# Early tile loads for the last gradient stage, one eviction moved from VectorE to ScalarE, and two stores freed of their order, in a gated linear-attention training kernel

## The chip, the cores and the metric

The kernel runs on one core of one Trainium2 chip. The metric is the device time of the execution in microseconds (us). The granted clock is the share of TensorE's full clock that the chip allows it, as the profile records it.

## The reference, cut to what matters

The reference is a forward pass and all its gradients. A gate `g` mixes two branches over `x` of 2048 rows and 640 columns: linear attention with 32 heads of 20, and a two-layer network with 1728 hidden columns.

```python
g = sigmoid((x * gate_w).sum(-1, keepdims=True))
a = linear_attention(x, wqkv) @ wo        # pq, pk = phi(q), phi(k); kv = pk^T v; z = sum pk
b = relu(x @ w1) @ w2                     # o = (pq kv) / (pq z + 1e-6)
out = g * a + (1 - g) * b
out, vjp = jax.vjp(f, x, wqkv, wo, w1, w2, gate_w)
return (out, *vjp(grad_out))              # d x, d wqkv, d wo, d w1, d w2, d gate_w
```

## The kernel before

The program is a sequence of phases over 16 tiles of 128 rows: 1 (k, v and the attention state), 2 (q, both branches, the output `po`), 3 and 4 (gradients of `w2` and `wo`, mixed with the attention gradient), 5 (hidden gradient), 6 (gradient of `w1`), 7 (gradients of q, k, v and of `x`), 8 (gradients of `wqkv` and of the gate). A scheduler orders the instructions of each engine, and buffers come from pools. An eviction (`evac`) copies a result that TensorE left in a PSUM buffer to an SBUF buffer, on ScalarE (`act`) or on VectorE (`dve`). A buffer of a released pool is used again by a later pool, and the later one then waits for the last use of the earlier one.

The end of a tile in phase 2. Three DMA transposes of the hidden tile and one of the attention tile leave as a burst, and the stores wait until the burst has landed:

```python
gT_ins = nc.sync.dma_start_transpose(goT[:], go_t[:])          # last of the four transposes
...
s1 = nc.gpsimd.dma_start(qkv_d[ts_, 0:D], pq_s[:])
tc.add_manual_dep(s1.ins, gT_ins.ins.name, sync_, reason="stores after the tile's transposing DMA burst")
s2 = nc.gpsimd.dma_start(go_d[ts_, :], go_t[:])
...
s3 = nc.gpsimd.dma_start(o_out[ts_, :], o_sb[:])
if t + 1 in lastT_p2:
    tc.add_manual_dep(s3.ins, lastT_p2[t + 1].ins.name, sync_, ...)
```

Phase 6, and the start of a tile in phase 7 (`p7_stage1`). Phase 7 has three stages, one tile apart each; stage 2 is the long one, with 30 matmuls into `pdx`:

```python
# phase 6, for each of five column blocks m
pw = ps4.tile([P, 2048], F32, tag="b4")
...                                                    # 64 matmuls
o_sb = w6p.tile([P, F], BF)
nc.scalar.copy(o_sb[:, 0:1024], pw[:, 0:1024])
nc.vector.tensor_copy(o_sb[:, 1024:F], pw[:, 1024:F])
nc.gpsimd.dma_start(out_4[m * P:(m + 1) * P, :], o_sb[:])
...
# phase 7
w7s = p7.enter_context(tc.tile_pool(name="w7s", bufs=2, side="right"))
w7p = p7.enter_context(tc.tile_pool(name="w7p", bufs=3, side="right"))
def p7_stage1(t):
    qkv_t = w7p.tile(...); nc.sync.dma_start(qkv_t[:], qkv_d[ts_, :])
    dndT_t = w7p.tile(...); nc.sync.dma_start(dndT_t[:], dndT_d[t])
    ...                                                # 6 transposes of k into PSUM: ppk
    evac("act", pkT[:], ppk[:])
    ...                                                # 6 transposes of v into PSUM: pvt
    evac("dve", vT[:], pvt[:])
    nc.vector.tensor_scalar(ep[:], qkv_t[:, 0:2 * D], -EPS, 1.0, ALU.add, ALU.min)
    ...                                                # pdq = dndT KVZt, pdv = pkT dKVz, pdk = vT dKVzt
    nc.vector.tensor_tensor(dq_t[:, 0:D], pdq[:, 32:32 + D], ep[:, 0:D], ALU.mult)
    nc.scalar.copy(dq_t[:, 2 * D:3 * D], pdv[:, 32:32 + D])
    nc.vector.tensor_tensor(dq_t[:, D:2 * D], pdk[:, 32:32 + D], ep[:, D:2 * D], ALU.mult)
def p7_stage1b(t): ...                                 # 15 transposes of dq_t (pt_, pt), evicted to dqT
def p7_stage2(t): ...                                  # pdx: 30 matmuls, then dx_sb and its store
p7_stage1(0); p7_stage1(1); p7_stage1b(0)
for t in range(NT):
    if t + 2 < NT: p7_stage1(t + 2)
    if t + 1 < NT: p7_stage1b(t + 1)
    p7_stage2(t)
```

## Time and profile before

| | |
|---|---|
| time, 4 runs | 802.33 us median, 800.47 to 805.8 |
| profiled run | 800.47 us, of which 798.8 us from the first to the last instruction |
| TensorE busy | 724.2 us, 91% of the span |
| phase 7, tile after tile | 6.953 us each |
| from the last matmul to the end | 20.4 us |

In the lines of a profile PE is TensorE and PEld its weight loads, DVE is VectorE, ACT is ScalarE, POOL is GpSimd, SPq is the queue of transfers that SyncE issues, and L602 is line 602 of the kernel. The first parts of the profile's page show busy time, the busy tenths in 40 slices of the span, and the share of each engine in the chain of work that ended last.

```profile
PE 724.2 (91%) x5410; PEld 426.2 (53%) x5507; DVE 311.0 (39%) x603; ACT 181.9 (23%) x291; POOL 94.9 (12%) x232
...
PE   2898999999999888999998999999987999999990
PEclk9999999999999999999998999999999999999996
...
PE 71%; DVE 6%; DMA 4%; issue 4%; ACT 3%; POOL 1%; SPq 1%; another core or an unknown queue 0%; POOLq 0%; ACTq 0%
```

TensorE is the limit nearly everywhere. The row of tenths shows where it is least so: the start, the two slices with 8 and 7 around the entry into phase 7 (slices 30 and 31, from about 580 us to 620 us), and the last slice, in which TensorE does nothing. Six other slices have an 8. The Trainium skill ("Perfetto Trace Analysis", the section on identifying performance opportunities) says to look for the gaps on the most-contended engine and for what ends them. This is the list of TensorE's waits (in all, times, longest, in us), cut:

```profile
PE pxt L186 <- DMA xs<-in_A_x_dram: 14.6, 3, 6.0
PE pdv L649 <- ACT pkT L79: 5.1, 15, 0.5
PE pdv L649 <- DVE dqkv L656: 4.0, 1, 4.0
...
PE ppk L629 <- DVE o_sb L602: 2.0, 1, 2.0
```

The first line is the wait for the first `x` at the start. The other three lie in phase 7: a small wait in every tile, and two waits at its entry. The timeline of the entry shows the second and third (start, length, engine, line, what; in brackets the idle time before it and what ended it):

```profile
595.67 0.49 PE L629 MATMUL ppk<-ident,qkv_t 128*120 128x128 bf16 x6 [2.03 <-DVE o_sb L602]
...
595.91 0.55 POOL L603 DMA_DIRECT2D out_dram<-o_sb  x1 [2.01 <-DVE o_sb L602]
...
600.44 1.56 DVE L638 TENSOR_SCALAR ep<-qkv_t 128x1280 f32<-128x1280 bf16 x2 [1.29 <-DMA out_dram<-o_sb]
...
602.79 0.69 PE L649 MATMUL pdv<-dKVz,pkT 120*128 120x120 bf16 x6 [3.95 <-DVE dqkv L656]
```

Read it from the bottom. TensorE waits 3.95 us for `dqkv`, which VectorE can only make after `ep`, and `ep` starts when the last store of phase 6 has landed. That store was issued at 595.91. `ep` needs nothing that the store writes: its buffer lies over the `o_sb` that is being stored. The inputs of phase 7 are not what is missing, as the first of these two issues on the DMA queue shows:

```profile
540.11 0.33 SPq L623 DMA_DIRECT2D qkv_t<-qkv_d  x1
...
593.67 3.18 SPq L699 DMA_DIRECT2D xs<-in_A_x_dram  x7
```

The first load of phase 7 leaves at 540 us, during phase 6, and 55 us before TensorE uses it. The second line begins the loads of `x` for phase 8. They run beside the last `o_sb` store, which takes 4.5 us to land (595.91 to 600.44), where the page gives a median of 2.7 us for the five stores of its kind.

A tile in the middle of phase 7:

```profile
641.27 0.80 ACT L79 COPY pkT<-ppk 120x768 bf16<-120x768 bf16 x1 [3.80 <-PE ppk L629]
...
641.62 0.55 DVE L81 COPY vT<-pvt 121x768 bf16<-121x768 bf16 x1
...
642.12 0.47 PE L649 MATMUL pdv<-dKVz,pkT 120*128 120x120 bf16 x6 [0.32 <-ACT pkT L79]
...
642.43 0.44 PE L653 MATMUL pdk<-dKVzt,vT 121*128 121x120 bf16 x6
```

`pkT` and `vT` are evicted side by side, `vT` is done before `pkT`, and TensorE waits 0.32 us, for `pkT` alone.

### The profile page before, as it was taken

The numbers are of one execution on the slowest core, as the hardware profiler recorded it, in microseconds if no ns is written. First come the engines' busy times: TensorE is split into PE (matmuls) and PEld (weight loads), VectorE is DVE, ScalarE is ACT, GpSimd is POOL, SyncE is SP. The second block draws the span as 40 slices with busy tenths as digits, with TensorE's granted clock in tenths as the row PEclk, the third lists the DMA queues.
The fourth block names the chain that finished last, engine by engine and source line by source line (L and its number), as shares of the span: only waits on it lengthen the run. The fifth ranks groups of instructions, "written<-read, shape, count | busy, mean of one in ns | idle before, by whom it ended". The sixth has DMA issues, their size and how long they took to land.

```text
span 798.8 us, 13034 instructions
## 1 busy us (share of the span) xinstructions
PE 724.2 (91%) x5410; PEld 426.2 (53%) x5507; DVE 311.0 (39%) x603; ACT 181.9 (23%) x291; POOL 94.9 (12%) x232
## 2 busy tenths in 40 slices
PE   2898999999999888999998999999987999999990
PEld 1555555555555565555554555555555666654440
DVE  0465735354363143333542555420017665520100
ACT  1444433232332163222210000000023333310100
POOL 3111021111111102222200000000000111100100
PEclk9999999999999999999998999999999999999996
DMA  9962154534535743222137444466127443100100
GB/s 301 311 205 105 38 126 90 117 92 89 112 91 113 249 130 99 75 76 79 42 89 161 81 88 90 75 146 177 45 89 238 132 126 114 47 30 25 49 25 25
DMA packets 124078, 87.75 MB, mean 110 GB/s; under 512 B 95105, under 2 KB 116194, under 8 KB 124018
## 3 DMA queue, kind: packets, MB, share of 16 engines
q1 hardware_dynamic: 115874, 59.03, 30.2%
q0 software_dynamic: 7424, 27.05, 9.8%
q8 instruction: 43, 0.70, 0.4%
q10 hardware_dynamic: 720, 0.82, 0.3%
q14 instruction: 17, 0.14, 0.1%
HBM read 37.94 MB, written 26.88 MB: 81 GB/s over the span
## 4 chain that ended last, share of the span: by engine, by line
PE 71%; DVE 6%; DMA 4%; issue 4%; ACT 3%; POOL 1%; SPq 1%; another core or an unknown queue 0%; POOLq 0%; ACTq 0%
PE pw L707 8%; PE pw L599 7%; PE po L347 7%; PE h1c L304 7%; PE pdx L557 6%; PE pdx L679 6%; PE dc L545 6%; PE pacc L434 3%; PE po L348 2%; PE pdx L680 2%; PE pdo L464 2%; PE pdx L558 2%; ACT pkT L79 1%; PE pacc L435 1%; DVE prod L467 1%
## 5 line engine op out<-in xcount | busy, mean ns | idle before, releaser
L557 PE MATMUL pdx<-W1T,dh1T 128*128 128x512 bf16 x215 | 63.8, 392 | 3.3 <-DMA W1T<-in_B_w_dram 3.3
L707 PE MATMUL pw<-dqkv,xs 128*128 128x512 bf16 (+1 forms) x314 | 64.7, 366 | 1.2 <-DVE dx_sb L682 0.9
L434 PE MATMUL pacc<-ds,hrs 128*128 128x512 bf16 (+1 forms) x209 | 60.9, 379 | 3.6 <-ACT o_sb L79 1.9
L679 PE MATMUL pdx<-WqkvT,dqT 128*128 128x512 bf16 x224 | 64.1, 379 | 0.0
L304 PE MATMUL h1c<-W,xT 128*128 128x512 bf16 (+1 forms) x311 | 61.3, 344 | 0.3
L545 PE MATMUL dc<-W2T,doutT 128*128 128x512 bf16 (+1 forms) x314 | 60.4, 345 | 0.3
L347 PE MATMUL po<-W_win,hrsT 128*128 128x512 bf16 x209 | 59.7, 379 | 0.0
L599 PE MATMUL pw<-hrs,xs 128*128 128x512 bf16 (+1 forms) x313 | 58.2, 345 | 1.3 <-DVE dxB L561 1.0
L680 PE MATMUL pdx<-WqkvT,dqT 128*128 128x128 bf16 x240 | 52.6, 219 | 0.8
L558 PE MATMUL pdx<-W1T,dh1T 128*128 128x128 bf16 x224 | 50.1, 224 | 0.5
L435 PE MATMUL pacc<-ds,hrs 128*128 128x128 bf16 (+1 forms) x224 | 49.1, 219 | 0.8
L348 PE MATMUL po<-W_win,hrsT 128*128 128x128 bf16 x224 | 49.0, 219 | 0.8
L707 PEld LDWEIGHTS <-xs 128*128 128x128 bf16 x320 | 31.3, 98 | 34.5 <-issue 1.0
L601 ACT CAST o_sb<-pw 128x1024 bf16<-128x1024 f32 x5 | 5.1, 1012 | 180.4 <-DMA dndT_t<-dndT_d 137.7
L599 PEld LDWEIGHTS <-xs 128*128 128x128 bf16 x320 | 30.1, 98 | 29.5 <-issue 1.1
L545 PEld LDWEIGHTS <-doutT 128*128 128x128 bf16 x320 | 29.9, 98 | 29.7
L304 PEld LDWEIGHTS <-xT 128*128 128x128 bf16 x320 | 28.9, 97 | 26.1
L546 DVE TENSOR_TENSOR hrs<-dc,msk 128x512 bf16<-128x512 f32 x64 | 37.3, 604 | 13.6 <-PE dc L545 13.6
L467 DVE TENSOR_TENSOR prod<-pdo,go 128x640 f32<-128x640 f32 x16 | 13.2, 822 | 68.8 <-PE pdo L465 68.8
L557 PEld LDWEIGHTS <-dh1T 128*128 128x128 bf16 x224 | 22.5, 101 | 30.3 <-issue 6.8
L679 PEld LDWEIGHTS <-dqT 128*128 128x128 bf16 x240 | 23.5, 98 | 26.6
L347 PEld LDWEIGHTS <-hrsT 128*128 128x128 bf16 x224 | 21.9, 98 | 24.7
(191 smaller groups left out, 1224.8 us busy)
## 6 DMA issues: line engine op xcount, KB each, us to landing
qkv_t<-qkv_d SPq DMA_DIRECT2D x16, 501.5 KB, 4.1
xs<-in_A_x_dram SPq DMA_DIRECT2D x48, 160.0 KB, 3.8
qkv_d<-kv_t POOLq DMA_DIRECT2D x16, 341.5 KB, 2.6
out_dram<-o_sb POOLq DMA_DIRECT2D x34, 160.0 KB, 2.3
dndT_d<-dndT_t POOLq DMA_DIRECT2D x16, 189.0 KB, 2.4
dndT_t<-dndT_d SPq DMA_DIRECT2D x16, 189.0 KB
ds<-in_grad_out_dram SPq DMA_DIRECT2D x16, 160.0 KB, 4.2
qkv_d<-pq_s POOLq DMA_DIRECT2D x16, 160.0 KB, 2.2
```

Source lines behind the costliest of these rows:

```text
L304: nc.tensor.matmul(h1c[:, 0:b_ - a_], xT[:, k, ts_], W1[:, k, a_:b_], start=(k == 0), stop=(k == KD - 1))
L347: nc.tensor.matmul(po[:, 0:512], lhsT, rhs[:, 0:512], start=(i == 0), stop=(i == nk - 1))
L348: nc.tensor.matmul(po[:, 512:D], lhsT, rhs[:, 512:D], start=(i == 0), stop=(i == nk - 1))
L434: nc.tensor.matmul(pacc[0:m, 0:512], lhsT, dS[t][:, 0:512], start=(t == 0), stop=(t == NT - 1))
L435: nc.tensor.matmul(pacc[0:m, 512:D], lhsT, dS[t][:, 512:D], start=(t == 0), stop=(t == NT - 1))
L545: nc.tensor.matmul(dc[:, 0:b_ - a_], doutT[:, k, ts_], W2T[:, k, a_:b_], start=(k == 0), stop=(k == KD - 1))
L557: nc.tensor.matmul(pdx[:, 0:512], dh1T[:, i, :], W1T[:, i, 0:512], start=(i == 0), stop=(i == NF - 1))
L558: nc.tensor.matmul(pdx[:, 512:D], dh1T[:, i, :], W1T[:, i, 512:D], start=(i == 0), stop=(i == NF - 1))
L599: nc.tensor.matmul(pw[:, a:b], xS[t][:, m * P:(m + 1) * P], hrs[t][:, a:b], start=(t == 0), stop=(t == NT - 1))
L679: nc.tensor.matmul(pdx[:, 0:512], dqT[:, i, :], WqkvT[:, i, 0:512], start=(i == 0), stop=(i == 14))
L680: nc.tensor.matmul(pdx[:, 512:D], dqT[:, i, :], WqkvT[:, i, 512:D], start=(i == 0), stop=(i == 14))
L707: nc.tensor.matmul(pw[:, a:b], xS[t][:, m * P:(m + 1) * P], dqkv[t][:, a:b], start=(t == 0), stop=(t == NT - 1))
```

## The change

Its intent: start the loads of the first three tiles of phase 7 before phase 6 (a pool of their own, opened earlier); relieve VectorE, the busier of the two evicting engines in phase 7; and let the last stores of phase 2 leave without waiting for the last tile's transposes. A fourth, tiny edit computes `1 - g` instead of `e * g`. The diff, cut to its core:

```diff
-        nc.vector.tensor_tensor(omg_all[:], e_g[:], g_all[:], ALU.mult)
+        nc.vector.tensor_scalar(omg_all[:], g_all[:], -1.0, 1.0, ALU.mult, ALU.add)
 ...                                                        # phase 2
-            tc.add_manual_dep(s1.ins, gT_ins.ins.name, sync_, reason="stores after the tile's transposing DMA burst")
+            if t < NT - 1:
+                tc.add_manual_dep(s1.ins, gT_ins.ins.name, sync_, reason="stores after the tile's transposing DMA burst")
 ...
-            if t + 1 in lastT_p2:
+            if t + 1 in lastT_p2 and t + 1 < NT - 1:
                 tc.add_manual_dep(s3.ins, lastT_p2[t + 1].ins.name, sync_, reason="stores after the next tile's transposing DMA burst")
 ...                                                        # before phase 6
+    w7l = tc.alloc_tile_pool(name="w7l", bufs=3, side="right")
+    loaded5 = {}
+    def load5(t):
+        qkv_t = w7l.tile([P, D + KVW], BF, tag="qkv_t")
+        nc.sync.dma_start(qkv_t[:], qkv_d[t * P:(t + 1) * P, :])
+        dndT_t = w7l.tile([WIN + 6, NW, P], BF, tag="dndT_t")
+        nc.sync.dma_start(dndT_t[:], dndT_d[t])
+        loaded5[t] = (qkv_t, dndT_t)
 ...                                                        # after the 16 loads of x for phase 6
+    for t in range(min(3, NT)):
+        load5(t)
 ...                                                        # phase 7, stage 1
-            qkv_t = w7p.tile([P, D + KVW], BF, tag="qkv_t")
-            nc.sync.dma_start(qkv_t[:], qkv_d[ts_, :])
-            dndT_t = w7p.tile([WIN + 6, NW, P], BF, tag="dndT_t")
-            nc.sync.dma_start(dndT_t[:], dndT_d[t])
+            if t not in loaded5:
+                load5(t)
+            qkv_t, dndT_t = loaded5.pop(t)
 ...
-            evac("dve", vT[:], pvt[:])
+            evac("act", vT[:], pvt[:])
```

More of the change, by code (lines that the diff above doesn't have):

```diff
@@ L309, in p2_stage1 @@
             hrsT = w2p.tile([P, NF, P], BF, tag="hrsT", bufs=3)
-            nosync_ = mybir.DependencyInfo(mybir.DependencyClass.NoSync, mybir.DependencyReason.DATA)
-            sync_ = mybir.DependencyInfo(mybir.DependencyClass.Sync, mybir.DependencyReason.DATA)
             hT0 = nc.sync.dma_start_transpose(hrsT[:, 0:8, :], hrs_t[:, 0:1024])
@@ L315, in p2_stage1 @@
             tc.add_manual_dep(hT1.ins, hT0.ins.name, nosync_, reason="burst order")
-            hT_last = nc.sync.dma_start_transpose(hrsT[:, 13, :], hrs_t[:, 1600:1728])
-            tc.add_manual_dep(hT_last.ins, hT1.ins.name, nosync_, reason="burst order")
+            hT2 = nc.sync.dma_start_transpose(hrsT[:, 13, :], hrs_t[:, 1600:1728])
+            tc.add_manual_dep(hT2.ins, hT1.ins.name, nosync_, reason="burst order")
             goT = w2p.tile([P, KD, P], BF, tag="goT", bufs=3)
             gT_ins = nc.sync.dma_start_transpose(goT[:], go_t[:])
-            tc.add_manual_dep(gT_ins.ins, hT_last.ins.name, nosync_, reason="keep the tile's transposing DMAs in one burst")
+            tc.add_manual_dep(gT_ins.ins, hT2.ins.name, nosync_, reason="burst order")
             lastT_p2[t] = gT_ins
@@ L606 @@
     if stop_after == "p5m":
+        w7l.release()
         dxBp.release()
@@ L694 @@
             p7_stage2(t)
+    w7l.release()
     xsp = tc.alloc_tile_pool(name="xsp2", bufs=NT, side="left")
```

## The prediction

> **What bounds the kernel.** TensorE: on the page it is busy 724.2 of 798.8 us, and the chain of waits gives it 71%. The list of what TensorE waits for sums to only about 45 us; 14.6 are the first x loads, which the change does not touch. So the change can win only a few us of named waits.
>
> **1. Early phase-7 loads: worth 0.** The timeline of the DMA queue shows that the first three qkv_t and dndT_t loads of the kernel before are already issued at 540.1 to 543.6 us, 50 us before phase 7 starts (593.4): the scheduler had hoisted them, since nothing in phase 6 held them back. The built order of the changed kernel has them at the same place in the queue (after the 16 xs loads, before the second xs loads). What stalls TensorE on entry is other: 2.0 us for the eviction of the last phase-6 accumulator (o_sb), then 4.0 us (593 to 609 timeline) for dqkv, which waits for ep, which waits for the store of the last phase-6 o_sb to land (600.4), because ep's buffer overlies that o_sb. In the changed build ep still overlies that buffer and waits for the same store. So the 6 us stay.
>
> **2. vT eviction from VectorE to ScalarE: costs about 3 us.** It takes 0.55 us on VectorE (547 ns) and should take as long as pkT's, 0.80 us on ScalarE, an estimate from the same shape. (The Trainium skill, "VectorE: DVE Perf Modes", section on the errata, gives PSUM-to-SBUF as 120 + FD/Accel cycles for VectorE and 172 + FD/Accel for ScalarE; for 768 bf16 elements, 0.53 and 0.78 us, so this trace agrees.) VectorE was not the limit (12.6 of 20 us busy). Before, pkT and vT were evicted side by side and TensorE waited 0.32 us per tile (for pkT). After, vT starts when pkT ends: in the tile at 640.6, pkT ends 642.07, vT would end about 642.95. The scheduler has moved six dqkv transposes ahead of the pdk matmuls, which fills from 642.43 to about 642.75. So pdk waits a further 0.2 to 0.3 us, in 14 steady tiles: +2.5 to +4 us. The period of 6.95 us becomes about 7.2.
>
> **3. Relaxed store order at the end of phase 2: worth 0, at most 1 us lost.** Only the stores of the last tile lose their wait: GpSimd's 6.9 us wait for goT (ending 264.2) goes. But TensorE waits for none of these stores. TensorE's 1.7 us there is for junk, on VectorE, unchanged. The earlier stores may share the DMA engines with the last transposes (3.3 us to landing), which have 1.4 to 2.3 us of slack before TensorE needs them.
>
> **Sum.** (omg as 1 - g swaps one small VectorE op for another: 0.) 802.3 + 0 + 3 + 0 = 805 us; range 800.5 to 808.5. Chances: faster by over 2% 0.01, within 2% 0.97, slower 0.02.
>
> **What would show it.** (1) TensorE's entry waits at about 593 to 603 the same, 2.0 and 4.0 us; first qkv_t loads near 540. (2) In the list of waits a new TensorE wait, pdk for vT on ScalarE, 0.2 to 0.3 us, 13 to 15 times; phase 7 (608.7 to 705) longer by about 3 us; vT on ScalarE at 0.80 us. (3) GpSimd's goT wait gone, TensorE unchanged around 255 to 285.
>
> **What would make it wrong.** ep not waiting for the store after all (up to 4 us won); the filling transposes covering vT entirely (0 lost); the earlier stores delaying the last transposes (1 to 3 us lost); run spread, 5 us among the four runs, as large as the effect.

## More of the kernel before

The end of phase 8, where the gradient of the gate is stored as a column of single elements:

```python
nc.gpsimd.dma_start(out_2[m * P:(m + 1) * P, :], o_sb[:, 0:3 * D])
with nc.allow_non_contiguous_dma(reason="dgate column"):
    nc.gpsimd.dma_start(out_6[m * P:(m + 1) * P].rearrange("(p o) -> p o", o=1), o_sb[:, 3 * D:3 * D + 1])
```

## The result, and the profile after

All ratios in this document are of one kernel's runs to the other's runs of the same rounds, and are not quite the ratios of the medians that stand beside them. Brackets give a 95% interval.

| kernel | median (lowest to highest), runs | ratio |
|---|---|---|
| before | 802.02 us (798.39 to 805.8), 16 | |
| after | 804.03 us (801.94 to 804.9), 11 | 1.0026 [1.0007, 1.0045] |

The changed kernel is the same within 2%, and a quarter of a per cent (2 us) slower. In the trace it is 801.1 us long instead of 798.8. The loss is in phase 7: phase 6 starts at 535.08 us in one trace and at 535.21 in the other, phase 8 at 713.33 and 715.51. The next two fences split phase 7 into stretches, for before and then after. Columns: the stretch and its length, busy time and count of PE, PEld, DVE, ACT and POOL, the granted clock, the DMA share and GB/s. The first line of each is the entry, to the fourth tile's transposes; the second is the next twelve tiles.

```profile
595.67:612.87 17.20, 12.32 (x150) 10.25 (x151) 11.07 (x16) 6.46 (x8) 0.97 (x4) 0.90 0.87 284
612.87:696.30 83.43, 78.90 (x890) 56.70 (x901) 49.67 (x71) 30.02 (x36) 8.82 (x24) 1.00 0.36 110
```

```profile
595.79:613.88 18.09, 14.18 (x149) 12.00 (x150) 9.49 (x13) 8.41 (x11) 0.97 (x4) 0.72 0.87 271
613.88:698.42 84.54, 79.73 (x890) 56.75 (x901) 44.11 (x59) 37.31 (x48) 8.83 (x24) 1.00 0.35 109
```

The entry takes 0.89 us longer, at a lower granted clock (0.72 instead of 0.90). The twelve tiles take 1.11 us longer at full clock, while VectorE has 5.6 us less to do in them and ScalarE 7.3 us more. The waits of TensorE have hardly moved:

```profile
PE pdv L660 <- ACT pkT L79: 5.1, 15, 0.6
...
PE pdv L660 <- DVE dqkv L667: 3.3, 1, 3.3
...
PE ppk L640 <- DVE o_sb L613: 2.0, 1, 2.0
```

The entry of the changed kernel has the same order as before:

```profile
596.03 0.55 POOL L614 DMA_DIRECT2D out_dram<-o_sb  x1 [2.01 <-DVE o_sb L613]
...
601.01 1.56 DVE L649 TENSOR_SCALAR ep<-qkv_t 128x1280 f32<-128x1280 bf16 x2 [5.27 <-DMA xs<-in_A_x_dram]
...
603.35 0.69 PE L660 MATMUL pdv<-dKVz,pkT 120*128 120x120 bf16 x6 [3.28 <-DVE dqkv L667]
```

The name in the middle line is another one, `xs` in place of `o_sb`. That is a caution for reading such lists: the releaser is inferred, and both transfers end in that stretch. Both kernels were built again to settle it. In both programs the first `ep` lies over the last `o_sb` and waits, among others, for the stores of the last two `o_sb` of phase 6 and for its own `qkv_t`, and for no load of `xs`. The experiment `ep_apart` below tests what that wait costs.

The loads leave at the same time as before (540.50 us in place of 540.11):

```profile
540.50 0.38 SPq L590 DMA_DIRECT2D qkv_t<-qkv_d  x1
```

And a tile in the middle:

```profile
642.56 0.80 ACT L79 COPY pkT<-ppk 120x768 bf16<-120x768 bf16 x1 [3.80 <-PE ppk L640]
...
643.25 0.81 ACT L79 COPY vT<-pvt 121x768 bf16<-121x768 bf16 x1
...
643.41 0.47 PE L660 MATMUL pdv<-dKVz,pkT 120*128 120x120 bf16 x6 [0.33 <-ACT pkT L79]
...
643.73 0.49 PE L677 MATMUL pt__6904<-ident,dqkv 128*128 128x128 bf16 x6
...
644.12 0.46 PE L664 MATMUL pdk<-dKVzt,vT 121*128 121x120 bf16 x6
```

`vT` now comes behind `pkT` on ScalarE and ends at 643.25 + 0.81 = 644.06, and `pdk` starts 0.06 us later. In between TensorE does six transposes of the tile before, which the scheduler moved there. No wait of `pdk` appears in the list, because the transposes fill nearly all of it. The tile period is 7.022 us instead of 6.953.

At the end of phase 2, GpSimd's wait for `goT` is gone. The store of `pq_s`, which waited 6.90 us for it before (the line is shown under `relax` below), leaves as soon as `pq_s` is made, ahead of the transpose at 263.70:

```profile
259.91 0.60 POOL L326 DMA_DIRECT2D qkv_d<-pq_s  x1 [0.90 <-DVE pq_s L81]
```

### The profile page after: what moved, and what is told of

Its sections match the earlier page's. It is cut to its first block, busy times and chain, and to the rows that moved or that the text cites. A ratio compares the mean times of both kernels' runs of the same rounds, so it can differ in the third digit from the quotient of the medians.

```text
span 801.1 us, 13058 instructions
## 1 busy us (share of the span) xinstructions
PE 726.3 (91%) x5410; PEld 428.8 (54%) x5507; DVE 303.3 (38%) x587; ACT 191.9 (24%) x307; POOL 94.9 (12%) x232
## 4 chain that ended last, share of the span: by engine, by line
PE 70%; DVE 6%; issue 4%; DMA 4%; ACT 3%; POOL 1%; another core or an unknown queue 0%; SPq 0%; POOLq 0%; ACTq 0%; DVEq 0%
PE pw L719 8%; PE pw L610 7%; PE h1c L304 7%; PE po L346 7%; PE pdx L690 6%; PE pdx L556 6%; PE dc L544 6%; PE pacc L433 3%; PE po L347 2%; PE pdx L691 2%; PE pdo L463 2%; PE pdx L557 2%; ACT pkT L79 1%; DMA wst<-in_B_w_dram 1%; DMA W1T<-in_B_w_dram 1%
## 5 line engine op out<-in xcount | busy, mean ns | idle before, releaser
L304 PEld LDWEIGHTS <-xT 128*128 128x128 bf16 x320 | 29.0, 97 | 26.0
L202 PEld LDWEIGHTS <-xT 128*128 128x128 bf16 x240 | 23.4, 101 | 22.3 <-issue 7.2
```

What stands on the lines that cost most here:

```text
L304: nc.tensor.matmul(h1c[:, 0:b_ - a_], xT[:, k, ts_], W1[:, k, a_:b_], start=(k == 0), stop=(k == KD - 1))
```

## The experiments

Twelve kernels ran. Kernels are compared only within the same rounds. All twelve gave the right result.

The theory after the result: the early loads are worth nothing, because the scheduler issued them early already; the move of `vT` is the loss; the freed stores are worth nothing or cost a little; and what holds up the entry is the overlaid buffer of `ep`. The rivals: the early loads or the freed stores do something that the move of `vT` hides, or the whole difference is scatter.

### The change taken apart: vt_act, after_vt_dve, prefetch, relax

Four kernels, five rounds each, on one chip with the same runs of before (802.76 us median of 11).

`vt_act` is the kernel before with this line alone:

```diff
-            evac("dve", vT[:], pvt[:])
+            evac("act", vT[:], pvt[:])
```

> The kernel before with only the vT eviction moved to ScalarE. Theory (the vT move is the whole loss: about 0.07 us in each of 13 steady phase-7 tiles, because pdk waits for a vT that ScalarE finishes last, plus about 0.5 to 1 us at the entry of phase 7): tile period 7.02 us (before 6.955), time ratio to before about 1.002 (+1 to +2.5 us). Rival (the loss comes from the prefetch pool or the relaxed stores): tile period 6.955, ratio 1.000.

`after_vt_dve` is the changed kernel with that line turned back:

```diff
-            evac("act", vT[:], pvt[:])
+            evac("dve", vT[:], pvt[:])
```

> The changed kernel with only vT back on VectorE. Theory: tile period back to 6.955 us, ratio to before 1.000 (within 0.15%). Rival (prefetch or store order costs time): ratio stays at about 1.0026, though the tile period is 6.955.

`prefetch` is the kernel before with the pool and the early loads alone:

```diff
+    w7l = tc.alloc_tile_pool(name="w7l", bufs=3, side="right")
 ...
+    for t in range(min(3, NT)):
+        load5(t)
```

> The kernel before with only the early loads (new pool). Theory: worth 0, since the scheduler had already put those loads at 540 us; first qkv_t load again near 540 us, the entry waits of TensorE again 2.0 and about 4 us, tile period 6.955, ratio 1.000 (within 0.15%). Rival (the early loads win the entry stall, and something else loses more): the 4 us wait shrinks, ratio 0.995 to 0.998.

`relax` is the kernel before with the freed stores alone:

```diff
+            if t < NT - 1:
+                tc.add_manual_dep(s1.ins, gT_ins.ins.name, sync_, ...)
 ...
-            if t + 1 in lastT_p2:
+            if t + 1 in lastT_p2 and t + 1 < NT - 1:
```

> The kernel before with only the store waits of the last phase-2 tile taken away. Theory: GpSimd's 6.9 us wait for goT at the end of phase 2 goes, TensorE's times from the first po matmul to the first phase-4 matmul stay at 167.8 us (within 0.2), ratio 1.000. Rival (the early stores collide with the last transposes): that stretch grows by 0.5 us or more.

| kernel | median us | ratio to before | entry, us | steady tile, us | first to last `po` matmul in phase 2, us |
|---|---|---|---|---|---|
| before (trace of the 800.47 us run) | 802.76 | | 17.20 | 6.953 | 166.16 |
| after (trace of the 802.89 us run) | see above | 1.0026 | 18.09 | 7.022, one 7.30 | 166.16 |
| vt_act | 805.34 | 1.0022 [1.0000, 1.0043] | 18.01 | 7.021, one 7.30 | 166.16 |
| after_vt_dve | 803.63 | 1.0011 [0.9986, 1.0036] | 17.77 | 6.950 | 166.64 |
| prefetch | 803.02 | 0.9998 [0.9978, 1.0018] | 18.05 | 6.951 | 166.18 |
| relax | 804.96 | 1.0022 [0.9998, 1.0045] | 18.34 | 6.953 | 168.01 |

The entry is from the first `ppk` matmul of the first tile to that of the fourth; the steady tile is the distance of two such matmuls after that. The last column runs from the start of the first `po` matmul to the end of the last.

By the clock alone the parts can't be told apart: each interval is 3 to 4 us wide, and the whole effect is 2 us; `relax` is as slow as `vt_act`. The traces tell more, because the steady tile responds to `vT` alone and the last column to the freed stores alone. These are the twelve steady tiles of `vt_act`, and then of `after_vt_dve`:

```profile
616.76:701.29 84.53, 79.73 (x890) 56.74 (x901) 44.14 (x59) 37.31 (x48) 9.03 (x24) 1.00 0.36 109
```

```profile
612.90:696.30 83.40, 78.90 (x891) 56.72 (x901) 49.73 (x71) 30.02 (x36) 8.81 (x24) 1.00 0.36 110
```

- The steady tile is 7.02 us in the two kernels with `vT` on ScalarE, and 6.95 us in the four with it on VectorE. Over the twelve tiles the move costs 84.54 - 83.43 = 1.1 us: 0.07 us in each, and 0.3 us more in one. In that one tile (it starts at 677.08 us in the changed kernel) `pkT` on ScalarE started after the transposes of v, not after those of k, and TensorE waited 0.60 us in place of 0.33. It is the same tile in both kernels. What holds `pkT` back in it is not settled.
- The early loads alone change nothing, in time or in the steady tile.
- The entry of 17.20 us in the trace of before is the shortest of six with `vT` on VectorE and the same phase 7: the others take 17.7 to 18.3 us (`dgate_row` and `relax_all` below, with 17.87 and 17.71, among them). So the 0.9 us which the changed kernel loses there can't be put down to `vT`: its 18.1 us is inside what the others take. It goes with the clock: TensorE ran at half clock for 3.4 us at the entry of before, for 6.8 us at the entries of the other five, and for 10.2 us at those of `vt_act` and after. That `vT` has no share in it isn't shown either: all four traces with `vT` on ScalarE (`vt_act_twice` and `fill_vt_act` below are the other two) have 10.2 us, and none of the other ten has more than 6.8. Over the whole of phase 7, the six with `vT` on VectorE take 117.7 to 118.8 us, 118.3 in the mean, and `vt_act` and after take 119.6 and 119.7. That is 1.4 us more, of which 1.1 lies in the twelve tiles.
- The Trainium skill ("TensorE: Matmul & The Clock Gate", Part 1) says that the clock gate which follows TensorE's activity has two levels, full and half, that its window of 3.41 us runs freely, and that its effect varies from run to run; the traces agree, with 3.4, 6.8 and 10.2 us at half clock at the entry, in stretches that begin in or after TensorE's idle times.
- The freed stores made one visible wait, in `relax`, at the very end of phase 2:

```profile
263.41 1.23 SPq L319 DMA_TRANSPOSE goT<-go_t  x1
...
268.46 0.39 PE L348 MATMUL po<-Wo_nat,goT 128*128 128x512 bf16 x1 [1.66 <-DMA goT<-go_t]
```

In the kernel before, the same transpose was issued at 261.02, and the store that waited for it could start at 264.19:

```profile
261.02 1.23 SPq L319 DMA_TRANSPOSE goT<-go_t  x1
...
264.19 0.60 POOL L328 DMA_DIRECT2D qkv_d<-pq_s  x1 [6.90 <-DMA goT<-go_t]
```

So it took at most 3.2 us to land before, and about 5 us with the stores beside it. It was also issued later: 5.4 us after the first transpose of its burst (258.04) in `relax`, and 4.4 us after it (256.65) in before. The expectation for `relax`, no change within 0.2 us, was missed: the stretch grew by 1.85 us, as the rival had it. The Trainium skill ("DMA: Bandwidth & Descriptors", the section that issuing engines are not separate DMA queues) says that DMAs of all issuing engines run on the same 16 DMA engines and interleave; this agrees. But it is one run: in the changed kernel, with the same freed stores, TensorE did not wait at all there, and in `after_vt_dve` 0.3 us. What decides it within a run was not found. So it is not shown that `vT` is the whole loss: the steady tiles hold 1.1 of the 2 us, and the freed stores may hold a part of the rest.

### Is vT really on the path? vt_act_twice

To see the mechanism and not just a difference of 0.07 us, `vT` was copied twice on ScalarE, one look.

```diff
-            evac("dve", vT[:], pvt[:])
+            evac("act", vT[:], pvt[:])
+            evac("act", vT[:], pvt[:])
```

> The kernel before with vT evicted on ScalarE, twice over (the second copy repeats the first; the result is right). Theory (in the steady tiles TensorE waits at pdk for vT, which is last in ScalarE's line): the tile period grows by about the 0.7 us of the second copy, less what two more transposes cover: 7.55 to 7.7 us. Rival (the 0.07 us come from the changed order of the TensorE instructions): the period stays at 7.0 to 7.1.

Measured: 820.82 us in the one run, and a tile period of 8.156 us. The wait that had been hidden is now in the list, and the timeline of a tile shows why it is larger than expected:

```profile
PE pdk L654 <- ACT vT L79: 16.0, 15, 1.1
```

```profile
641.68 0.81 ACT L79 COPY vT<-pvt 121x768 bf16<-121x768 bf16 x1
...
642.37 0.71 ACT L658 CAST dqkv<-pdv 128x640 bf16<-128x640 f32 x1
642.95 0.83 ACT L79 COPY vT<-pvt 121x768 bf16<-121x768 bf16 x1
...
643.84 0.46 PE L654 MATMUL pdk<-dKVzt,vT 121*128 121x120 bf16 x6 [1.08 <-ACT vT L79]
```

The expectation missed the size: the scheduler put the eviction of `pdv` between the two copies, so the second starts 1.27 us after the first and not 0.7. What the run does show is that `pdk` waits for `vT` on ScalarE as soon as the transposes no longer cover it. It also shows how close the changed kernel is to that edge.

### Where does the entry's time go? ep_apart

The two pools of phase 7's working buffers are opened before phase 6, so that neither `ep` nor anything else of phase 7 lies over an `o_sb`.

```diff
+    w7s = tc.alloc_tile_pool(name="w7s", bufs=2, side="right")
+    w7p = tc.alloc_tile_pool(name="w7p", bufs=3, side="right")
     with ExitStack() as p6:
 ...
-        w7s = p7.enter_context(tc.tile_pool(name="w7s", bufs=2, side="right"))
-        w7p = p7.enter_context(tc.tile_pool(name="w7p", bufs=3, side="right"))
```

> The kernel before with the phase-7 SBUF pools of ep and of the tiles allocated before phase 6, so that ep no longer lies over the phase-6 output buffer o_sb. Theory (the entry stall is the wait of ep for the landing of the last o_sb store, not for loads): ep runs near 545 us, TensorE's 4.0 us wait for dqkv at the entry goes, except for some tenths; the entry (first ppk to fourth ppk start, 17.2 us before) shortens by 3 to 4 us and the ratio to before is 0.995 to 0.997. Rival (the stall is a load arriving late, or VectorE's own work): the wait stays at 3 us or more, ratio 1.000.

Measured: 798.85 us against 804.23 of the same rounds, ratio 0.9937 [0.9914, 0.9959]. The entry is 13.73 us instead of 17.20, and the wait of `pdv` for `dqkv` is gone from the list. `ep` of the first tile is made 50 us before it is needed, and `dqkv` follows as soon as `pdq` is there:

```profile
543.48 0.83 DVE L638 TENSOR_SCALAR ep<-qkv_t 128x1280 f32<-128x1280 bf16 x1 [12.27 <-DMA qkv_t<-qkv_d]
...
593.19 0.81 DVE L656 TENSOR_TENSOR dqkv<-pdq,ep 128x640 bf16<-128x640 f32 x1
```

The clock shows 5 us, a little more than expected, and the trace 3.5; other traces of the old entry, at 17.7 to 18.3 us, would make it 4.0 to 4.6. The edit moved `ep` and the tiles' pool together; that `ep` is the one that counts is read from the trace.

So the idea of the change, to make ready for phase 7 during phase 6, was sound, but it was applied to the wrong buffers: the loads were early already, and the working buffers were not.

### Can phase 7 lose its wait for pkT altogether? fill, fill_vt_act

`fill` splits stage 1. The transposes of k and v of tile t+3 go into the middle of the 30 `pdx` matmuls of tile t, and the transposes of `dqkv` go between `pdq` and `pdv`. The evictions then have half of `pdx` to finish in.

```diff
-        p7_stage1(0)
-        if NT > 1:
-            p7_stage1(1)
-        p7_stage1b(0)
+        p7_stage1(0)
+        p7_stage1c(0)            # pdq, pdv, pdk and dqkv of the tile
+        p7_stage1(1)
+        p7_stage1c(1, 0)         # with the dqkv transposes of tile 0 behind its pdq
+        p7_stage1(2)
         for t in range(NT):
 ...
-            p7_stage2(t)
+            p7_stage2a(t)        # pdx, blocks 0 to 7
+            if t + 3 < NT:
+                p7_stage1(t + 3)
+            p7_stage2b(t)        # pdx, blocks 8 to 14
```

> The kernel before with the k and v transposes of the next tile put in the middle of the pdx matmuls, so that both evictions are done long before pdv and pdk need them, on VectorE and ScalarE as before. Theory (the steady loss of phase 7 is the 0.32 us wait for pkT, and more if vT is on ScalarE): that wait (5.1 us in 15 tiles) goes; the tile period falls from 6.955 to between 6.65 (no other wait) and 6.9 (a new wait for dx_sb or dqkv on VectorE); ratio 0.995 to 0.999. Rival (TensorE's rate sets the period and the wait is hidden): period 6.95, ratio 1.000.

Measured: 797.11 us against 804.23, ratio 0.9910 [0.9878, 0.9942]. The tile period is 6.553 us, 0.40 us less, and of the waits for `pkT` in the steady tiles none is left. Both numbers are better than expected. For the period the reason is in the trace: the list counts a wait from the recorded end of the matmul before it, 0.32 us, while from the start of that matmul to the start of the next it was 0.51 us, and is 0.06 in `fill`; a gap of 0.12 us instead of 0.05 between `pdk` and `pdx` takes a little of it back. For the ratio it is not settled: phase 7 is 4.1 us shorter than in the trace of before (113.60 against 117.66), and the clock says 7, with 4.7 at the edge of its interval.

```profile
633.40 0.80 ACT L80 COPY pkT<-ppk 120x768 bf16<-120x768 bf16 x1 [1.98 <-PE ppk L631]
...
636.51 0.46 PE L657 MATMUL pdv<-dKVz,pkT 120*128 120x120 bf16 x6
```

`pkT` is ready at 634.20, and is used at 636.51. In this kernel the move of `vT` can be tried again: `fill_vt_act` is `fill` with the one line of `vt_act`, one look.

> The refilled phase 7 with vT on ScalarE. Theory, that moving vT costs time only because pdv and pdk come right behind the evictions: with the evictions half a pdx ahead of their use it costs nothing, tile period 6.55 us as in the refilled kernel (6.553), no tile at 7.3. Rival, that ScalarE as an engine is the limit or that its copies hold up TensorE through the two PSUM buffers of pkT and vT: period 6.6 to 6.8.

Measured: 796.36 us in the one run, tile period 6.55 us in every steady tile, none at 7.3. So in this kernel ScalarE carries `vT` at no cost, because the eviction has time; the move costs where the next matmul stands right behind it. The rival, ScalarE's load, falls.

### The tail: dgate_row

This is not a part of the change. After the last matmul the kernel before runs for 20.4 us, in which nothing is computed after 780.5. The chain ends in the store of the gate's gradient, whose issue is the second of these two, and the page's list of DMA issues gives the time to landing as its last number (us, the median of five):

```profile
780.82 0.54 POOL L711 DMA_DIRECT2D out_dram<-o_sb  x1 [11.90 <-DVE o_sb L710]
781.36 0.54 POOL L713 DMA_DIRECT2D out_dram<-o_sb  x1
...
out_dram<-o_sb POOLq DMA_DIRECT2D x5, 0.2 KB, 15.3
```

256 bytes take 15.3 us, and they are 128 elements of two bytes. The Trainium skill ("DMA: Bandwidth & Descriptors", the section of rules for kernel authors) says that a DMA whose last dimension is not contiguous becomes one descriptor for each element, and advises to make it contiguous. `dgate_row` does so: the column of each of the five blocks goes to a small tile, and one transpose at the end turns it into five rows of 128.

```diff
-            with nc.allow_non_contiguous_dma(reason="dgate column"):
-                nc.gpsimd.dma_start(out_6[m * P:(m + 1) * P].rearrange("(p o) -> p o", o=1), o_sb[:, 3 * D:3 * D + 1])
+        dg_s = w8p.tile([P, KD], BF, tag="dg_s", bufs=1)
 ...                                                        # in the loop over m, in place of the two lines above
+            nc.scalar.copy(dg_s[:, m:m + 1], pw[:, 3 * D:3 * D + 1])
+        pdg = ps4.tile([P, P], BF, tag="b4")
+        nc.tensor.transpose(pdg[0:KD, :], dg_s[:], ident[:])
+        dg_r = w8p.tile([KD, P], BF, tag="dg_r", bufs=1)
+        nc.scalar.copy(dg_r[:], pdg[0:KD, :])
+        nc.sync.dma_start(out_6.rearrange("(m p) -> m p", p=P), dg_r[:])
```

> The kernel before with the five 128-row column stores of out_6 replaced by one store of five rows of 256 bytes, after a transpose at the end. Theory (the tail after TensorE's last matmul, 20 us, is the column store: 15.3 us from issue to landing): the tail falls to about 9 us, ratio 0.985 to 0.988. Rival (the tail is a fixed cost of the end of the program or of the large out_2 store): the tail stays above 17 us, ratio 0.998 to 1.000.

Measured: 789.91 us against 804.23, ratio 0.9830 [0.9805, 0.9855]. From the last matmul of `pw` to the end it takes 7.7 us instead of 20.4. The new store is the last line of the kernel's timeline, 4.7 us before the end:

```profile
782.89 0.28 SPq L718 DMA_DIRECT2D out_dram<-dg_r  x1
```

The edit does more than change the shape: one store takes the place of five, and it leaves from SyncE's queue and not from GpSimd's. Which of these counts was not taken apart.

### Is it the order of stores that protects phase 2? relax_all

The wait in `relax` left the question whether the order of stores after transposes earns its keep in all 16 tiles. `relax_all` is the kernel before without it:

```diff
-            tc.add_manual_dep(s1.ins, gT_ins.ins.name, sync_, reason="stores after the tile's transposing DMA burst")
 ...
-            if t + 1 in lastT_p2:
-                tc.add_manual_dep(s3.ins, lastT_p2[t + 1].ins.name, sync_, ...)
```

> Kernel before with the order of stores after transposes taken away for every tile of phase 2, not only at its end. Theory, that this order protects the transposes from sharing the DMA engines: as in the run with the relaxed stores at the end (goT 1.7 us late there once), many of the 16 tiles lose some tenths to 1.7 us; the stretch from the first to the last matmul of po grows from 166.2 by 3 to 15 us, with TensorE waits for goT and hrsT; ratio 1.004 to 1.02. Rival, that the one wait of 1.7 us was the end of phase 2 alone, where no later tile gives slack: the stretch stays within 166.2 to 168.0 us, ratio 1.000 to 1.002.

Measured: ratio 1.0021 [0.9988, 1.0055] over 3 rounds. The stretch from the first to the last `po` matmul is 166.49 us, 0.33 more than before, with one wait of 0.4 us for `goT`. The ratio alone decides nothing, since its interval reaches into both forecasts. By the trace, the one that there is, the theory of a protecting order falls, and the rival holds: with later tiles to hide in, the sharing costs nothing that TensorE feels. The wait of 0.4 us is in the last tile. Only this tile, with nothing behind it, is exposed, by 0 to 1.85 us in the four traces that have the freed stores at the end.

### All together: best, best_nosplit

`best` joins `ep_apart`, `fill` and `dgate_row` with one more edit, which keeps the accumulator of phase 6 in two pools of one buffer each, so that phase 7 can start while the last accumulator is still being evicted. `best_nosplit` is without that edit:

```diff
-        ps4 = p6.enter_context(tc.tile_pool(name="ps6", bufs=2, space=PSUM))
+        ps4s = [p6.enter_context(tc.tile_pool(name=f"ps6{c}", bufs=1, space=PSUM)) for c in "ab"]
 ...
-            pw = ps4.tile([P, 2048], F32, tag="b4")
+            pw = ps4s[m % 2].tile([P, 2048], F32, tag="b4")
```

> All three wins at once (ep's buffers apart from the last o_sb, phase 7 refilled so that pkT and vT are evicted during pdx, the gate column sent as one row), and the phase-6 accumulator in two pools. Theory that the three are in three different stretches and so add: 0.63% + 0.90% + 1.70% = 3.2% less, ratio 0.963 to 0.973, 776 to 783 us; entry into phase 7 about 13 to 15 us instead of 17 to 18, tile period 6.55, end of the last matmul to end of the span 8 us. Rival, that part of the fill's gain was already the entry's (the entry of the fill kernel was also shorter, 16.4 us) so that they overlap: ratio 0.973 to 0.980.

> The same without the two accumulator pools of phase 6. Theory: the first transposes of phase 7 then wait for the very last o_sb eviction, 2 us, as in the kernel before; slower than the kernel with two pools by 1 to 2 us (0.1 to 0.25%). Rival: the 2 us are hidden by nothing else but are replaced by the wait for the eviction that pdq has anyway, so both are equal within 0.5 us in the trace.

| kernel | median us | ratio to before (800.95) |
|---|---|---|
| best | 775.17 | 0.9679 [0.9648, 0.9710] |
| best_nosplit | 776.92 | 0.9695 [0.9665, 0.9726] |

Within the noise the three gains add: 0.9937 x 0.9910 x 0.9830 = 0.9680, and `best_nosplit`, which is the three and nothing else, has 0.9695. The product is uncertain by about 0.005, an estimate from the three intervals, so a small overlap isn't excluded. The entry of `best` is 11.0 us, shorter than the 13 to 15 that were expected, and its median is a little under the 776 us expected. The start of phase 7 in the trace of `best`:

```profile
592.78 0.50 PE L631 MATMUL ppk<-ident,qkv_t 128*120 128x128 bf16 x6
...
594.13 0.88 DVE L605 CAST o_sb<-pw 128x704 bf16<-128x704 f32 x1
```

The transposes now start before the last accumulator is evicted, and the 2.0 us wait is gone. It is back in the trace of `best_nosplit`:

```profile
PE ppk L631 <- DVE o_sb L605: 2.0, 1, 2.0
```

There phases 6 and 7 together take 169.02 us instead of 166.57 (178.24 before). By the clock the two differ by 0.16%, which is inside both intervals, so the worth of the two pools rests on the traces. In `best` no half clock was recorded at the entry.

## Why the prediction was right, and where a size was off

- The total. 805.0 us was predicted, in a range of 800.5 to 808.5, and 804.03 came, in the class that was given 0.97. The ground for a small effect, that only 45 us of TensorE's time are waits and that the change touches few of them, held.
- Step 1, the early loads: "worth 0". Right, and for the reason given. The loads were at 540 us in both kernels, the waits at the entry stayed (2.0, and 4.0 became 3.3), and `prefetch` alone is at 0.9998. That `ep` waits because its buffer lies over a stored one was an argument at first; `ep_apart` shows it, with 3.5 us less at the entry and the wait gone.
- Step 2, `vT` on ScalarE: "costs about 3 us", "2.5 to +4". The mechanism was right and the size was off. `vT` takes 0.81 us there, as estimated from the same shape. (The figures worked out in the prediction from the Trainium skill, "VectorE: DVE Perf Modes", section on the errata, 0.53 us for VectorE and 0.78 for ScalarE, are estimates: they take Accel as 2 for VectorE and as 1 for ScalarE. The trace has 0.55 and 0.80.) The term that was mis-sized is "pdk waits a further 0.2 to 0.3 us, in 14 steady tiles". The wait measured is 0.06 us. The estimate put the end of `vT` 0.88 us after the end of `pkT` (642.07 to 642.95). In the changed kernel `pkT` ends at 643.36 and `vT` at 644.06, 0.70 us later, since the second copy starts 0.1 us before the recorded end of the first. The filling transposes start at 643.73 and take 0.33 us, as predicted (0.32), so that they end when `vT` does. The 0.18 us by which `vT` came sooner is the better part of what the estimate had as a wait. The period came out as 7.02 us and not 7.2, the twelve steady tiles lost 1.1 us, and the named wait was not in the list; it appeared when the copy was doubled.
- Part of the remaining difference of the two traces, 0.9 us at the entry, was not in the prediction at all. It goes with more time at half clock. Five kernels with `vT` on VectorE lose 0.5 to 1.1 us there as well, so scatter is enough to explain it; whether `vT` has a small share is open.
- Step 3, the freed stores: "worth 0, at most 1 us lost". The sign was right: GpSimd's wait is gone, and no gain came of it. The bound was too tight: one trace of `relax` lost 1.85 us in that stretch (168.01 against 166.16), of which 1.66 was a wait for the transpose that now shared the DMA engines. It is what the prediction named among the things that could make it wrong. The other three traces with the freed stores lost 0, 0.3 and 0.5 us, a mean of 0.7 over the four.
- Step 4, `1 - g`: 0. It was not run alone. What it does by itself is not shown.
- The total came out near the middle partly by luck. Of the 2 us that the clock shows, 1.1 to 1.4 are traced to `vT`, for which 3 had been set; the rest can be the freed stores or scatter. The scatter of 5 to 7 us between runs is larger than all of these.

## What to carry to other kernels

Before moving loads earlier, look at when they are issued now, and at which wait ends last at the entry of the stage: here the loads were 55 us early, and a working buffer laid over a tile that was still being stored held up everything. Moving an eviction to the less busy engine is not a gain in itself; here it cost when the next matmul stood right behind it, and was free when the evictions were placed half a stage ahead. And read the end of the trace, where no engine is busy: the largest gain, 1.7%, came from five stores of 256 bytes each, columns that were sent as the rows of one store instead.

## What the Trainium skill lacked or had wrong

- "DMA: Bandwidth & Descriptors", anatomy of one DMA: the fit of 2.0 us plus bytes over the bandwidth has no term for the number of descriptors. For a store of 128 elements of two bytes it gives 2.0 us; the trace shows 15.3 us to landing (median of five). The page's rule against non-contiguous last dimensions has no such number beside it.
- "DMA: Bandwidth & Descriptors", rules for kernel authors: it says that a transpose next to ordinary DMAs needs nothing. That is about correct results. In time, a transpose with stores beside it took about 5 us to land in one run instead of at most 3.2, and TensorE waited 1.66 us.
- "TensorE: Matmul & The Clock Gate", the section on why this matters for your kernels, warns of idle gaps over about 3 us. In `ep_apart` a gap of 2.0 us (to 591.84), with transposes and small matmuls after it, was followed by half clock from 593.2 for 3.4 us. In `best`, without that gap, none was recorded at the entry.
- No page says how far an inferred releaser can be trusted. The same wait of `ep` was put down to the store of `o_sb` in one trace and to a load of `xs` in the other (601.01 us), although the program built has no wait of `ep` for `xs`.
